# Masks of a block-sparse attention made later, new step tables for the attention and the first expert, and two pieces of weight work moved: fp32 attention and two MoE layers in one launch

## The chip, the cores and the metric

One NeuronCore of one Trainium2 chip runs the whole program. The metric is the device time of one execution in microseconds (us). Engines: PE multiplies matrices, DVE (VectorE), ACT (ScalarE) and POOL (GpSimd) work on vectors, SP issues the DMAs.

## The reference, cut to what matters

```
# attention: B=2, H=8, S=768, D=64; block 32, window 16
k_sum = max over each block of 32 keys;  v_sum = mean over each block of 32 values
scores_l = q @ k.T / 8, kept where |i-j| < 16
scores_s = q @ k_sum.T / 8 + log(32)
a = softmax([scores_l, scores_s]);  x = a @ [v, v_sum]         # 1536 rows of 512
h = x @ w_in (512x2048);  g = h - tanh(h);  x2 = g @ w_out (2048x512)
out = ((x2 @ w1) * (x2 @ w2)) @ w3 @ w_out2                    # 1024 wide, then 512
```

All is float32, and the weights arrive as 64-bit numbers.

## The kernel before, in words

**Products.** A float32 product is made as three reduced-precision ones (`split_mm`, L237 to L240): high x high, high x low, low x high. So every operand has a high part (a cast, `wh`, by ACT L193 or POOL L191) and a low part (a subtraction on POOL, `wl`, L200). A weight first comes in by DMA as `raw` (L126), and ACT (L145, sometimes also L149, the units listed in `PLAN["SIGN"]`) and DVE (L152 to L162) turn its 64-bit numbers into `dec`.

**Attention, 0 to about 118 us.** 24 groups g of 4 query tiles are in flight at once, as a pipeline of steps: S scores on PE (L428), M0 to M3 row maxima with a mask added (DVE, L438), E0 to E3 exponentials (ACT, L443), R one over the row sum (DVE, L450 and L451), PP the scaling of the probabilities `pr` (POOL, L455), T four transposes (PE, L462), PB their copy `pt` (ACT, L467), V the values `av` (PE, L477), XH and XL the two parts of the result (ACT, DVE). Every third group brings new keys (`key_blocks`, K0 to K2, block maxima on DVE L370 to L377, copied into the keys on POOL, L379), new values (`value_blocks`, on PE, from the rows of `mean`), their rows `vr` (ACT, L399) and their DMA into `vg` (BR, L404). Between these, PE makes the 32 parts of w3 @ w_out2 ahead of time: W0 and W1, `w34a`, each part two halves of three matmuls of 512 columns; the numbers of parts per step are in `PLAN["N34"]`. The tokens H, L, D, U and ST are pieces of the weights' decoding (cast, low part, one DVE operation, a whole unit, start of a unit).

No scheduler orders any of this. Each engine runs its instructions in the order in which the program writes them, and one that waits holds up all behind it. For the attention that order is written in `PLAN["L"]`, three lists of (token, lag), one for the first two steps, one until step 17, one after; a step g runs each token for group g minus its lag. Ahead of the steps the program calls `key_blocks(0, .)` and `scores(0)`; ahead of those again POOL makes the `mean` rows (L267 to L281) and three masks (L282 to L292) out of `band` (L258 to L265).

**First MoE, about 118 to 375 us.** `hidden` (ph), tanh, and the way back (x), 48 times; `PLAN["MIDDLE"]` sets the order inside a step, and its last row holds for all later ones.

**Second MoE.** For the first of three token blocks a loop over m = 0 to 7 makes a = x2 @ w1 (`product_a`), b and c = a*b (`product_b`), the high and low part of w3 @ w_out2 (`w34_split(m)`: cast `w34h` on ACT, `w34l` on POOL) and then adds the output product of the m before (`final`). The other two token blocks are made together, in seven products of halves instead of eight, for pairs of m (`group`, called for w1 and then for w2). A group runs products 1, 6, 5, then, at each `next(g)`, the output product that is pending (`between`) and 7, then 2, 4 and 3. After each DVE adds the bank `p_w` into a11, a12, a21, a22 (L900). `w_sums` makes the sums of weights that the next group multiplies with: up to its first `yield` `t_w` (two additions on DVE), up to its second `s_w` (four half-size ones on DVE, two casts on ACT L937, two low parts on POOL L243).

Of the kernel before, what the change touches and what calls it, by code (L numbers as in the profile page):

```python
# [21 lines left out]
P = 128  # L22
# [4 lines left out]
QT = 64  # L27
# [22 lines left out]
ALL = 4  # L50
FLUSH = 4

PLAN = {"cuts": [2, 17], "N34": [0, 0, 0, 0, 0, 2, 0, 2, 2, 0, 2, 1, 2, 1, 2, 0, 1, 2, 3, 1, 2, 1, 1, 3, 1, 2, 3],
        "MORE": (15, 18, 22), "MOREU": (20, 24, 32),
        "SIGN": (1, 3, 5, 7, 9, 11, 13, 14, 15, 17, 19, 20, 21, 22, 23, 24, 26, 27, 28, 29, 32, 35, 39, 41, 43, 45, 47, 49, 51, 53, 55, 57, 59, 61, 63, 65, 67, 69, 71, 73, 75, 77, 79), "ACT": (0, 4, 7, 8, 16, 19, 22, 25, 27, 28, 29, 31, 33, 35)}
PLAN["L"] = [
# [14 lines left out]
]  # L71
PLAN["MIDDLE"] = [
# [9 lines left out]
]  # L82
NEG = -8.0 * 1000000000.0
# [6 lines left out]
def fused_kernel(tc, qT, kT, vW, w_in, w_out, w1, w2, w3, wo2, out):  # L90
# [156 lines left out]
    with tc.tile_pool(name="base", bufs=1) as base, \  # L247
# [12 lines left out]
        for hf in range(2):  # L260
# [2 lines left out]
                                    fill=NEG, base=-1, channel_multiplier=-1)  # L263
            nc.gpsimd.affine_select(out=part, in_=part, pattern=[[-1, WK]], compare_op=ALU.is_ge,
                                    fill=NEG, base=2 * WIN - 1, channel_multiplier=1)  # L265

        mean = base.tile([P, 6 + BLK], F32, name="mean")  # L267
        nc.gpsimd.memset(mean, 0.0)

        def rows(col, a, b):  # L270

            nc.gpsimd.memset(col, 1.0 / BLK)
            for base_, step in ((-a, 1), (b - 1, -1)):
                nc.gpsimd.affine_select(out=col, in_=col, pattern=[[0, 1]], compare_op=ALU.is_ge, fill=0.0,
                                        base=base_, channel_multiplier=step)

        rest = base.tile([P, 1], F32, name="mean_rest")
        rows(mean[:, 6:7], WIN, WIN + BLK)
        rows(mean[:, 7:8], WIN + BLK, QT)
        rows(rest, CW, CW + WIN)  # L280
        nc.gpsimd.tensor_tensor(out=mean[:, 7:8], in0=mean[:, 7:8], in1=rest, op=ALU.add)  # L281
        masks = []  # L282
        for z in range(3):
            mk = base.tile([P, NC], F32, name=f"mask{z}")
            nc.gpsimd.memset(mk[:, BC], LOG_BLK)
            nc.gpsimd.tensor_copy(out=mk[:, :QT], in_=band[:, :QT])
            nc.gpsimd.tensor_copy(out=mk[:, CW:], in_=band[:, QT:])
            if z == 0:
                nc.gpsimd.memset(mk[:, :WIN], NEG)
            if z == 2:  # L290
                nc.gpsimd.memset(mk[:, NC - WIN:], NEG)
            masks.append(mk)  # L292

        w34 = [base.tile([P, DM], F32, tag=f"w34_{i}", name=f"w34_{i}") for i in range(NM)]
        xh = [base.tile([P, KC, TB], F32R, name=f"xh_{k}") for k in range(NTB)]
# [43 lines left out]
        with tc.tile_pool(name="p1", bufs=1) as p1, \  # L339
# [74 lines left out]
            def scores(g):  # L414

                nonlocal n_s
                n, u = divmod(g, NU)
                st[g] = []
                for _ in range(1 + (g >= ALL)):
                    tag = "extra" if g >= ALL and n_s % 3 == 2 else "s"  # L420
                    n_s += g >= ALL
                    st[g].append(ps1.tile([P, TU, NC], F32, tag=tag, bufs=2 if tag == "s" else 1, name=f"s_{g}_{n_s}"))
                wt.one = g >= ALL
                for i in range(TU):
                    t = u * TU + i
                    for hf in range(2):
                        r = slice(hf * QT, (hf + 1) * QT)
                        mm(out=st[g][i % len(st[g])][half_of(g, i, hf), i, :], lhsT=qt[n][r, t * QT:(t + 1) * QT],  # L428
                           rhs=kt[n][r, t * CW:t * CW + NC], start=True, stop=True)
# [78 lines left out]
            for i in range(3):  # L508
                key_blocks(0, i)
            scores(0)  # L510
            n34 = 0
            NN = B * NP
            done = set()
# [264 lines left out]
        def product_a(m, k):  # L778
            ph = half("w1", m, k)
            a = tmp("u", f"a_{m}_{k}")  # L780
            nc.scalar.copy(out=a, in_=ph)
            return a
# [193 lines left out]
        for m in range(1, NM):  # L976
            wt.high()
            wt.low()
            wt.start(min(2, len(wt.free) - (1 if m > 5 else (6 - m) // 2)))
            if m == NM - 1:  # L980
                assert len(wt.t) == len(wt.units)
                wt.free += [(rawp, "raw", "raw", NRAW)] * NRAW
                _, lhs = w_sums("w1", 0)
            a = product_a(m, 0)
            wt.unit(1)
            pb = half("w2", m, 0)
            c = product_b(m, 0, a, pb)
            wt.unit(1)
            if m == 1:
                resplit(4)  # L990
                resplit(4)
            if m == 4:
                for i in range(H):
                    x_sums(i)
            if m == 5:
                for i in (5, 6):
                    x_split(i, 0, nc.vector)
                    x_split(i, 1, nc.vector)
                wt.free += [(px, f"x{k}{c}", f"x{k}{c + 1}", 1) for k, c in ((1, 0), (2, H))]
            if m > 2:  # L1000
                wt.high()
                wt.low()
            w34_split(m)
            final(*prev)
            prev = m, 0, c
        todo, last = [(*prev, range(TB // P))], []
# [18 lines left out]
        for m in range(0, NM, 2):  # L1025
            pl_a, a12, a21 = wt.take(f"a_{m}", F32)
            pl_b, a22, b22 = wt.take(f"ab_{m}", F32)
            g = group("w1", m, lhs, a11, a12, a21, a22)
            next(g)
            sums = w_sums("w2", m)  # L1030
            next(sums)
            next(g)
            lhs = next(sums)
            for _ in range(3):
                next(g, None)
            pl_c, b12, b21 = wt.take(f"b_{m}", F32)
            b11 = tmp("u", f"b11_{m}")
            g = group("w2", m, lhs, b11, b12, b21, b22)
            next(g)
            more = m + 2 < NM  # L1040
            if more:
                sums = w_sums("w1", m + 2)
                next(sums)
            for a, b in ((a22, b22), (a11, b11), (a21, b21)):
                next(g)
                if more and a is a22:
                    lhs = next(sums)
                tt(a, a, ALU.mult, b)
            next(g, None)
            tt(a12, a12, ALU.mult, b12)  # L1050
            todo += [split_c(a11, m, 1), split_c(a21, m + 1, 1)]
            last += [split_c(a12, m, 2), split_c(a22, m + 1, 2)]
            wt.free += [pl_a, pl_b, pl_c]
# [56 lines left out]
```

## Time and profile before

| | |
|---|---|
| three runs, us | 574.33, 574.31, 571.29; median 574.31 |
| the profiled execution, us | 572.8, of it 571.1 the span of the engines' work |
| busy, us of the span | PE 556.0 (97%), DVE 456.1 (80%), ACT 335.1 (59%), POOL 292.0 (51%) |
| the chain that ended last | PE 81%, DVE 9%, issue 3%, ACT 3%, DMA 2% |
| granted PE clock, mean | 0.997 of full speed |

All times below are from the one profiled execution, in us from the start of the span. The page's 40 slices show PE at 6 tenths in the first two slices (14.3 us each), at 9 or more in every other one but the last, which holds the last copies and the DMAs of the output. The granted clock is at 8 tenths in the second slice and at 9 or more in all others.

### The profile page before, as it was taken

The page shows a single profiled execution, that of the slowest core. Times are in us where ns is not written, and L with a number is a line of the kernel's source. Part 1 is how long each engine was busy: PE and PEld are TensorE (multiplying, and loading weights), DVE is VectorE, ACT ScalarE, POOL GpSimd, SP SyncE. Part 2 cuts the span into 40 slices and gives each one's busy share as a digit, 9 for nine tenths or more (in the row PEclk, how much of TensorE's full clock was granted, in tenths as well). Part 3 has the DMA queues.
Part 4 walks back from the last instruction along what each step waited for, and adds up shares of the span by engine and source line. Part 5 has one row for each costly group of instructions (what it writes and reads, how often), then busy time and mean ns, then how long its engine had stood idle before and what let it go on. Part 6 is the DMA issues. An engine that isn't in the chain of part 4 may idle for free.

```text
span 571.1 us, 9225 instructions
## 1 busy us (share of the span) xinstructions
PE 556.0 (97%) x3224; PEld 450.0 (79%) x3224; DVE 456.1 (80%) x880; ACT 335.1 (59%) x739; POOL 292.0 (51%) x257
## 2 busy tenths in 40 slices
PE   6699999999999999999999999999999999999997
PEld 5477777778888888888888888888788877888885
DVE  4878899998899999889999769999378677868510
ACT  4799888876978876577766667845233321213110
POOL 4766775834464655535645315466536653617220
PEclk9899999999999999999999999999999999999999
DMA  8998777441232332122223003222000100000021
GB/s 329 352 312 287 279 242 231 143 146 38 74 111 76 110 100 84 37 84 87 88 82 102 1 2 110 75 73 75 0 1 1 74 1 1 1 0 1 1 92 55
DMA packets 18526, 56.56 MB, mean 99 GB/s; under 512 B 1968, under 2 KB 4656, under 8 KB 18480
## 3 DMA queue, kind: packets, MB, share of 16 engines
q1 hardware_dynamic: 18336, 55.84, 29.6%
q8 instruction: 25, 0.41, 0.3%
q14 instruction: 21, 0.17, 0.1%
q10 hardware_dynamic: 144, 0.13, 0.1%
HBM read 51.64 MB, written 3.15 MB: 96 GB/s over the span
## 4 chain that ended last, share of the span: by engine, by line
PE 81%; DVE 9%; issue 3%; ACT 3%; DMA 2%; SPq 1%; POOL 0%; DVEq 0%; ACTq 0%
PE ph L238 7%; PE ph L239 7%; PE ph L240 7%; PE x L238 7%; PE x L239 7%; PE x L240 7%; PE p_w L238 5%; PE p_w L240 5%; PE p_w L239 4%; PE o L240 4%; PE o L239 4%; PE o L238 4%; PE w34a L238 2%; DMA raw<-wo 2%; PE w34a L239 2%
## 5 line engine op out<-in xcount | busy, mean ns | idle before, releaser
L243 POOL TENSOR_TENSOR gl<-g,gh 128x512 fp32r<-128x512 f32 x48 | 65.0, 1354 | 127.1 <-ACT gh L729 69.4
L200 POOL TENSOR_TENSOR wl<-dec,wh 128x512 fp32r<-128x512 f32 x72 | 111.7, 1553 | 18.1 <-ACT wh L193 14.5
L238 PE MATMUL x<-gh,wh 128*128 128x512 f32 x192 | 74.9, 390 | 0.0
L238 PE MATMUL ph<-xh,wh 128*128 128x512 f32 x192 | 74.8, 390 | 0.0
L239 PE MATMUL x<-gl,wh 128*128 128x512 f32 x192 | 74.7, 389 | 0.0
L240 PE MATMUL ph<-xh,wl 128*128 128x512 f32 x192 | 74.7, 389 | 0.0
L239 PE MATMUL ph<-xl,wh 128*128 128x512 f32 x192 | 74.7, 389 | 0.0
L240 PE MATMUL x<-gh,wl 128*128 128x512 f32 x192 | 74.7, 389 | 0.0
L707 ACT ACTIVATE u<-ph 128x512 f32<-128x512 f32 x48 | 28.8, 600 | 52.0 <-PE ph L240 52.0
L162 DVE SCALAR_TENSOR_TENSOR dec<-raw,dec 128x512 uint32<-128x512 uint32 x48 | 48.6, 1013 | 1.5
L718 DVE TENSOR_TENSOR g<-ph,u 128x512 f32<-128x512 f32 x48 | 33.0, 687 | 17.6 <-ACT th L708 16.1
L720 DVE SCALAR_TENSOR_TENSOR g<-sq,g 128x512 f32<-128x512 f32 x48 | 45.3, 943 | 0.6 <-ACT sq L713 0.5
L243 POOL TENSOR_TENSOR s_w<-s_w,s_w 128x512 fp32r<-128x512 f32 x16 | 23.1, 1460 | 42.9 <-ACT s_w L937 23.2
L193 ACT CAST wh<-dec 128x512 fp32r<-128x512 f32 x54 | 33.7, 624 | 15.9 <-DVE dec L162 15.7
L238 PEld LDWEIGHTS x<-gh,wh 128*128 128x128 f32 x192 | 36.1, 188 | 7.9 <-DVE x2a L755 0.4
L443 ACT ACTIVATE pr<-pr,nm 128x120 f32<-128x120 f32 x96 | 37.9, 401 | 7.2 <-DVE nm L438 7.2
L240 PEld LDWEIGHTS x<-gh,wl 128*128 128x128 f32 x192 | 36.0, 188 | 7.5
L238 PEld LDWEIGHTS ph<-xh,wh 128*128 128x128 f32 x192 | 36.0, 188 | 7.5
L239 PEld LDWEIGHTS ph<-xl,wh 128*128 128x128 f32 x192 | 36.1, 188 | 7.4
L240 PEld LDWEIGHTS ph<-xh,wl 128*128 128x128 f32 x192 | 36.0, 188 | 7.5
L239 PEld LDWEIGHTS x<-gl,wh 128*128 128x128 f32 x192 | 36.0, 188 | 7.5 <-POOL gl L243 0.2
L724 DVE COPY_PREDICATED g<-mk,ph 128x512 f32<-128x512 uint32 x48 | 36.0, 749 | 3.9
(164 smaller groups left out, 1426.8 us busy)
## 6 DMA issues: line engine op xcount, KB each, us to landing
raw<-w SPq DMA_DIRECT2D x32, 512.0 KB
raw<-w_in SPq DMA_DIRECT2D x16, 512.0 KB
raw<-w_out SPq DMA_DIRECT2D x16, 512.0 KB
vg<-vW SPq DMA_DIRECT2D x8, 768.0 KB
raw<-wo SPq DMA_DIRECT2D x8, 512.0 KB
kt<-kT SPq DMA_DIRECT2D x7, 544.0 KB
qt<-qT SPq DMA_DIRECT2D x7, 384.0 KB
out<-u_out SPq DMA_DIRECT2D x6, 256.0 KB
```

The lines of the kernel that those rows point to most:

```text
L162: lambda tu=tu, su=su, lo=lo: stt(out=tu, in0=lo, scalar=29, in1=su, op0=ALU.logical_shift_right, op1=ALU.bitwise_or)])
L193: nc.scalar.copy(out=h, in_=self.t[n])
L200: nc.gpsimd.tensor_tensor(out=l, in0=self.t[self.n_low], in1=h[:, :].bitcast(F32), op=ALU.subtract)
L238: mm(out=acc, lhsT=lh, rhs=rh, start=start, stop=False)
L239: mm(out=acc, lhsT=lh, rhs=rl, start=False, stop=False)
L240: mm(out=acc, lhsT=ll, rhs=rh, start=False, stop=stop)
L243: eng.tensor_tensor(out=out, in0=x, in1=high.bitcast(F32), op=ALU.subtract)
L443: nc.scalar.activation(out=pr[g][:, i, :], in_=pr[g][:, i, :], func=AF.Exp, scale=-1.0, bias=nm[g][:, i:i + 1], accum_out=z[g][:, i, :1])
L707: nc.scalar.activation(out=u, in_=ph, func=AF.Square)
L718: nc.vector.tensor_tensor(out=gn, in0=ph, in1=u, op=ALU.mult)
L720: nc.vector.scalar_tensor_tensor(out=gn, in0=sq, scalar=GAM, in1=gn, op0=ALU.add, op1=ALU.mult)
L724: nc.vector.copy_predicated(out=gn, mask=mask[:, :].bitcast(U32), data=ph)
```

## The change

Four things. The masks and the rows of `mean` are made by the same POOL instructions, behind `key_blocks(0, .)` and `scores(0)` instead of ahead of them. The tables of `PLAN` are new: all three lists of `L`, the second cut (18 instead of 17), `N34`, `SIGN`, `ACT`, `MORE`, `MOREU` and the first eight rows of `MIDDLE`. `w34_split(m)` runs right behind `product_a` in the m loop, and the two calls ahead of its old place are gone. And in a group for w1, the sums for w2 begin behind the second `next(g)` instead of the first. The number of instructions of each kind stays, but for one more unit that is listed in `SIGN` (one ACT operation more, one DVE operation fewer).

```diff
-PLAN = {"cuts": [2, 17], "N34": [0, 0, 0, 0, 0, 2, 0, 2, 2, 0, 2, 1, 2, 1, 2, 0, 1, 2, 3, 1, 2, 1, 1, 3, 1, 2, 3],
+PLAN = {"cuts": [2, 18], "N34": [0, 0, 0, 0, 0, 1, 1, 2, 2, 0, 2, 1, 1, 1, 3, 0, 2, 1, 3, 0, 3, 1, 1, 3, 1, 2, 3],
...
@@ -264,33 +265,6 @@
             nc.gpsimd.affine_select(out=part, in_=part, pattern=[[-1, WK]], compare_op=ALU.is_ge,
                                     fill=NEG, base=2 * WIN - 1, channel_multiplier=1)
 
-        mean = base.tile([P, 6 + BLK], F32, name="mean")
-        nc.gpsimd.memset(mean, 0.0)
-
-        def rows(col, a, b):
-
-            nc.gpsimd.memset(col, 1.0 / BLK)
-            for base_, step in ((-a, 1), (b - 1, -1)):
-                nc.gpsimd.affine_select(out=col, in_=col, pattern=[[0, 1]], compare_op=ALU.is_ge, fill=0.0,
-                                        base=base_, channel_multiplier=step)
-
-        rest = base.tile([P, 1], F32, name="mean_rest")
-        rows(mean[:, 6:7], WIN, WIN + BLK)
-        rows(mean[:, 7:8], WIN + BLK, QT)
-        rows(rest, CW, CW + WIN)
-        nc.gpsimd.tensor_tensor(out=mean[:, 7:8], in0=mean[:, 7:8], in1=rest, op=ALU.add)
-        masks = []
-        for z in range(3):
-            mk = base.tile([P, NC], F32, name=f"mask{z}")
-            nc.gpsimd.memset(mk[:, BC], LOG_BLK)
-            nc.gpsimd.tensor_copy(out=mk[:, :QT], in_=band[:, :QT])
-            nc.gpsimd.tensor_copy(out=mk[:, CW:], in_=band[:, QT:])
-            if z == 0:
-                nc.gpsimd.memset(mk[:, :WIN], NEG)
-            if z == 2:
-                nc.gpsimd.memset(mk[:, NC - WIN:], NEG)
-            masks.append(mk)
-
         w34 = [base.tile([P, DM], F32, tag=f"w34_{i}", name=f"w34_{i}") for i in range(NM)]
         xh = [base.tile([P, KC, TB], F32R, name=f"xh_{k}") for k in range(NTB)]
         xl = [base.tile([P, KC, TB], F32R, name=f"xl_{k}") for k in range(NTB)]
@@ -508,6 +482,32 @@
             for i in range(3):
                 key_blocks(0, i)
             scores(0)
+            masks = []
+            for i in range(3):
+                mk = base.tile([P, NC], F32, name=f"mask{i}")
+                nc.gpsimd.memset(mk[:, BC], LOG_BLK)
+                nc.gpsimd.tensor_copy(out=mk[:, :QT], in_=band[:, :QT])
+                nc.gpsimd.tensor_copy(out=mk[:, CW:], in_=band[:, QT:])
+                if i == 0:
+                    nc.gpsimd.memset(mk[:, :WIN], NEG)
+                if i == 2:
+                    nc.gpsimd.memset(mk[:, NC - WIN:], NEG)
+                masks.append(mk)
+            mean = base.tile([P, 6 + BLK], F32, name="mean")
+            nc.gpsimd.memset(mean, 0.0)
+
+            def rows(col, a, b):
+
+                nc.gpsimd.memset(col, 1.0 / BLK)
+                for base_, step in ((-a, 1), (b - 1, -1)):
+                    nc.gpsimd.affine_select(out=col, in_=col, pattern=[[0, 1]], compare_op=ALU.is_ge, fill=0.0,
+                                            base=base_, channel_multiplier=step)
+
+            rest = base.tile([P, 1], F32, name="mean_rest")
+            rows(mean[:, 6:7], WIN, WIN + BLK)
+            rows(mean[:, 7:8], WIN + BLK, QT)
+            rows(rest, CW, CW + WIN)
+            nc.gpsimd.tensor_tensor(out=mean[:, 7:8], in0=mean[:, 7:8], in1=rest, op=ALU.add)
             n34 = 0
             NN = B * NP
             done = set()
@@ -982,6 +982,7 @@
                 wt.free += [(rawp, "raw", "raw", NRAW)] * NRAW
                 _, lhs = w_sums("w1", 0)
             a = product_a(m, 0)
+            w34_split(m)
             wt.unit(1)
             pb = half("w2", m, 0)
             c = product_b(m, 0, a, pb)
@@ -997,10 +998,6 @@
                     x_split(i, 0, nc.vector)
                     x_split(i, 1, nc.vector)
                 wt.free += [(px, f"x{k}{c}", f"x{k}{c + 1}", 1) for k, c in ((1, 0), (2, H))]
-            if m > 2:
-                wt.high()
-                wt.low()
-            w34_split(m)
             final(*prev)
             prev = m, 0, c
         todo, last = [(*prev, range(TB // P))], []
@@ -1027,9 +1024,9 @@
             pl_b, a22, b22 = wt.take(f"ab_{m}", F32)
             g = group("w1", m, lhs, a11, a12, a21, a22)
             next(g)
+            next(g)
             sums = w_sums("w2", m)
             next(sums)
-            next(g)
             lhs = next(sums)
             for _ in range(3):
                 next(g, None)
```

The new tables move instructions at these places. POOL at the start; `kt` is the keys with their block maxima, which the first scores read, `band` is what the masks are cut from, `pr` the probabilities. Before:

```order
L285 MEMSET mask_111 128x24
L286 COPY mask_111<-band 128x64
L287 COPY mask_111<-band 128x32
L291 MEMSET mask_111 128x16
L379 COPY kt_156<-kb_176 128x12x24
L455 TENSOR_TENSOR pr_189<-pr_189,r_248 128x480
```

Of the change:

```order
L265 AFFINE_SELECT band<-band 64x96
L263 AFFINE_SELECT band<-band 64x96
L265 AFFINE_SELECT band<-band 64x96
L353 COPY kt_129<-kb_149 128x12x24
L488 MEMSET mask_161 128x24
L489 COPY mask_161<-band 128x64
L490 COPY mask_161<-band 128x32
```

The copy of the first block maxima, which stood behind the last mask, now stands ahead of the first.

PE around the transposes T(3), with `w34a_0` and `w34a_1` the two halves of the first part of w3 @ w_out2, which come behind the second values V(1). Before:

```order
L477 MATMUL av_445<-pt_344,vg_164 64x64 x8
L238 MATMUL w34a_0_460<-wh_294,wh_321 128x512
L239 MATMUL w34a_0_460<-wl_295,wh_321 128x512
L240 MATMUL w34a_0_460<-wh_294,wl_322 128x512
L238 MATMUL w34a_1_464<-wh_294,wh_321 128x512
L239 MATMUL w34a_1_464<-wl_295,wh_321 128x512
L240 MATMUL w34a_1_464<-wh_294,wl_322 128x512
L462 MATMUL t_476<-ident,pr_311 120x128 x4
L428 MATMUL s_5_492<-kt_211,qt_274 64x120 x2
```

Of the change:

```order
L451 MATMUL av_440<-pt_343,vg_137 64x64 x8
L436 MATMUL t_455<-ident,pr_314 120x128 x4
L239 MATMUL w34a_0_461<-wh_284,wh_323 128x512
L240 MATMUL w34a_0_461<-wl_285,wh_323 128x512
L241 MATMUL w34a_0_461<-wh_284,wl_324 128x512
L239 MATMUL w34a_1_465<-wh_284,wh_323 128x512
L240 MATMUL w34a_1_465<-wl_285,wh_323 128x512
L241 MATMUL w34a_1_465<-wh_284,wl_324 128x512
L402 MATMUL s_5_485<-kt_209,qt_307 64x120 x2
```

T(3) moves from behind the part to ahead of it.

POOL between PP(1) (`pr_207`, after: `pr_204`) and PP(3) (`pr_311`, after: `pr_314`), with the casts and low parts of the first four decoded weights. Before:

```order
L455 TENSOR_TENSOR pr_207<-pr_207,r_291 128x480
L200 TENSOR_TENSOR wl_295<-dec_214,wh_294 128x512
L191 CAST wh_321<-dec_266 128x512
L200 TENSOR_TENSOR wl_322<-dec_266,wh_321 128x512
L455 TENSOR_TENSOR pr_245<-pr_245,r_337 128x480
L191 CAST wh_392<-dec_316 128x512
L200 TENSOR_TENSOR wl_393<-dec_316,wh_392 128x512
L191 CAST wh_414<-dec_362 128x512
L455 TENSOR_TENSOR pr_311<-pr_311,r_411 128x480
```

Of the change:

```order
L429 TENSOR_TENSOR pr_204<-pr_204,r_291 128x480
L201 TENSOR_TENSOR wl_285<-dec_214,wh_284 128x512
L192 CAST wh_323<-dec_260 128x512
L192 CAST wh_340<-dec_319 128x512
L429 TENSOR_TENSOR pr_244<-pr_244,r_345 128x480
L201 TENSOR_TENSOR wl_324<-dec_260,wh_323 128x512
L201 TENSOR_TENSOR wl_341<-dec_319,wh_340 128x512
L192 CAST wh_413<-dec_389 128x512
L429 TENSOR_TENSOR pr_314<-pr_314,r_418 128x480
```

Of the same work, two low parts instead of one now stand between PP(2) and PP(3).

## Rows read from the trace of the kernel before

**Rows 1.** Busy time by stage, all engines: PE, PEld, DVE, ACT, POOL, clock, DMA
```profile
20.00:30.00 10.00, 7.08 (x87) 5.38 (x88) 8.78 (x36) 8.08 (x32) 7.71 (x9) 0.83 1.02 339
60.00:80.00 20.00, 19.23 (x246) 14.47 (x246) 17.29 (x69) 18.65 (x64) 13.63 (x16) 1.00 0.77 264
200.00:300.00 100.00, 100.00 (x442) 82.51 (x441) 93.44 (x131) 69.69 (x123) 51.38 (x34) 1.00 0.27 81
```

**Rows 2.** Timeline of the first 12 us: start, length, engine, what, [idle before]
```profile
5.12 0.20 DVE L377 TENSOR_REDUCE kb<-hb 128x24 f32<-128x48 f32 x1
6.40 0.42 POOL L379 COPY kt<-kb 128x288 f32<-128x288 f32 x1
6.88 4.89 PE L428 MATMUL s<-kt,qt 64*64 64x120 f32 x48 [2.10 <-POOL kt L379]
```

**Rows 3.** The chain that ended last, then the timeline: what the first values wait for
```profile
6.80 12.26 DMA raw<-wo
...
19.31 0.69 PE L477 MATMUL av<-pt,vg 120*64 120x64 f32 x16 [0.64 <-DMA vg<-vr]
```

**Rows 4.** Timeline 21 to 30 us, POOL, then PE, around T(3)
```profile
21.61 0.99 POOL L455 TENSOR_TENSOR pr<-pr,r 128x480 f32<-128x480 f32 x1 [1.07 <-DVE r L451]
24.72 0.61 POOL L191 CAST wh<-dec 128x512 fp32r<-128x512 f32 x1
26.23 1.27 POOL L200 TENSOR_TENSOR wl<-dec,wh 128x512 fp32r<-128x512 f32 x1
...
26.20 0.80 PE L238 MATMUL w34a<-wh,wh 128*128 128x512 f32 x1
28.76 0.60 PE L462 MATMUL t<-ident,pr 128*120 128x128 f32 x4
```

**Rows 5.** PE and its granted clock, microsecond by microsecond
```profile
25.00:26.00 1.00, 0.86 (x16) 0.56 1.03 391
...
28.00:29.00 1.00, 1.00 (x6) 0.73 1.21 178
```

**Rows 6.** Timeline of PE: W then T then S; T then W then S
```profile
47.41 0.50 PE L238 MATMUL w34a<-wh,wh 128*128 128x512 f32 x1
...
48.92 0.60 PE L462 MATMUL t<-ident,pr 128*120 128x128 f32 x4
49.45 0.64 PE L428 MATMUL s<-kt,qt 64*64 64x120 f32 x16
...
95.79 0.65 PE L462 MATMUL t<-ident,pr 128*120 128x128 f32 x4
96.20 0.48 PE L238 MATMUL w34a<-wh,wh 128*128 128x512 f32 x1
...
97.77 0.64 PE L428 MATMUL s<-kt,qt 64*64 64x120 f32 x16
```

**Rows 7.** Timeline of PE at one output product that waits for w34l
```profile
406.65 0.39 PE L238 MATMUL o<-w34h,gh_c 128*128 128x512 f32 x1
407.22 0.50 PE L239 MATMUL o<-w34l,gh_c 128*128 128x512 f32 x1 [0.18 <-POOL w34l L243]
```

**Rows 8.** Timeline of PE, DVE, PE and POOL in the second pair's group for w1
```profile
472.98 0.39 PE L240 MATMUL p_w<-xh,s_w 128*128 128x512 f32 x1
...
472.98 1.75 DVE L900 TENSOR_TENSOR t_w<-wh,wl 128x512 f32<-128x512 f32 x2
...
474.65 0.68 DVE L900 TENSOR_TENSOR a<-a,p_w 128x512 f32<-128x512 f32 x1
...
475.70 0.39 PE L240 MATMUL p_w<-xh,wl 128*128 128x512 f32 x1
...
476.10 0.50 PE L238 MATMUL p_w<-xh,s_w 128*128 128x512 f32 x1
...
477.57 2.55 POOL L243 TENSOR_TENSOR s_w<-s_w,s_w 128x512 fp32r<-128x512 f32 x2 [4.00 <-ACT s_w L937]
...
478.96 0.40 PE L238 MATMUL p_w<-t,s_w 128*128 128x512 f32 x1
```

More of the change, by code (lines that the diff above doesn't have):

```diff
@@ L51 @@
 FLUSH = 4
-PLAN = {"cuts": [2, 17], "N34": [0, 0, 0, 0, 0, 2, 0, 2, 2, 0, 2, 1, 2, 1, 2, 0, 1, 2, 3, 1, 2, 1, 1, 3, 1, 2, 3],
-        "MORE": (15, 18, 22), "MOREU": (20, 24, 32),
-        "SIGN": (1, 3, 5, 7, 9, 11, 13, 14, 15, 17, 19, 20, 21, 22, 23, 24, 26, 27, 28, 29, 32, 35, 39, 41, 43, 45, 47, 49, 51, 53, 55, 57, 59, 61, 63, 65, 67, 69, 71, 73, 75, 77, 79), "ACT": (0, 4, 7, 8, 16, 19, 22, 25, 27, 28, 29, 31, 33, 35)}
+PLAN = {"cuts": [2, 18], "N34": [0, 0, 0, 0, 0, 1, 1, 2, 2, 0, 2, 1, 1, 1, 3, 0, 2, 1, 3, 0, 3, 1, 1, 3, 1, 2, 3],
+        "MORE": (15, 18, 22, 23, 24), "MOREU": (5, 13, 15, 20, 22, 25, 26),
+        "SIGN": (1, 2, 3, 5, 6, 7, 9, 11, 13, 15, 17, 18, 19, 20, 21, 22, 23, 24, 25, 27, 28, 29, 30, 31, 33, 34, 35, 37, 38, 39, 41, 43, 45, 47, 49, 51, 53, 55, 57, 59, 61, 63, 65, 67, 69, 71, 73, 75, 77, 79), "ACT": (0, 4, 8, 9, 16, 20, 22, 25, 26, 27, 29, 30, 31, 33)}
 PLAN["L"] = [
[14 rows of a table removed]
[15 rows of a table added]
 ]
 PLAN["MIDDLE"] = [
[8 rows of a table removed]
[8 rows of a table added]
     ["HID", "ST", "H", "EV", "C", "U", "UT", "G", "SM", "MM", "L", "RS", "BK"],
```

45 rows, old and new, of the table PLAN are left out of this document.

## Prediction

> **What bounds the kernel now.** First the page's table by engine and its 40 slices: PE is busy 97% of the span of 571.1 us, and all slices but the first two and the last stand at 9 tenths or more. So there is little to win, and the question is where PE still stands still, or does the same work in more time. Next the busy time by stage [rows 1]. The long middle gives the yardstick: between 200 and 300 us PE has 442 matmuls in 100 us, 0.226 us for one of 512 columns, with no idle time. From 20 to 30 us PE is idle 2.92 us, at a mean granted clock of 0.83; from 60 to 80 us it is idle 0.77, and there ACT is busy 18.65 of 20, so ACT is nearly a second bound. Then the timeline of the first 12 us [rows 2], the chain of waits and what the first values wait for [rows 3], the timeline around T(3) [rows 4], and the clock microsecond by microsecond [rows 5]. Last the timeline of PE at a few switches between kinds of work [rows 6], at one output product [rows 7] and in a group of seven products [rows 8].
>
> The sum is made against the profiled execution, 572.8, which lies 1.5 below the median of 574.31 and 1.5 above the lowest run, 571.29. Its mean with the three runs is 573.2, and that is what I carry the sum over to.
>
> **Masks and rows of means behind the block maxima.** The last block maximum is ready at 5.12 + 0.20 = 5.32 us, POOL copies it into the keys only at 6.40, and S(0) starts at 6.88, after a wait for that copy [rows 2]. All of 6.40 - 5.32 = 1.08 us is masks and mean rows, which go behind it. So S(0) comes up to 1.08 earlier. What takes it back: the third raw block is issued at 6.80 and lands 12.26 later, at 19.06, and the first values, behind it in the order of ACT and of the DMAs, start at 19.31 after a wait for their rows [rows 3]. In the new order of SP the same bytes are asked for in nearly the same order (one keys' and one values' transfer change places), and ACT still decodes that block ahead of the exponentials of groups 2 and 3. I therefore count **0** for the head start itself, with ends of 0 and -1.08. If that cover (the block's arrival) were gone, the whole 1.08 would show.
>
> **T(3) ahead of the first part of w34.** PE leaves V(1) at about 26.20 and goes into that part at once; T(3) runs at 28.76 [rows 4]. With the change T(3) comes first and waits for PP(3). POOL's PP(2) ends at 21.61 + 0.99 = 22.60. Behind it, up to PP(3), stood a cast, a low part and a cast; now two low parts and a cast: 22.6 + 2 x 1.27 + 0.61 + 0.99 = 26.7, and 0.2 for what PP(2) itself may start later, 26.9 for the end of PP(3) [rows 4]. So PE stands still from 26.20 to about 26.9, 0.7 us, and works without a gap from there. What it loses was cheap time: the clock was granted at 0.56 between 25 and 26 and at 0.73 between 28 and 29 [rows 5], so at or near its lower level, 1.2 GHz, in between, and the six matmuls of the part took 28.76 - 26.20 = 2.56 instead of 6 x 0.226 = 1.36 [rows 1, 4]. At half the rate 0.7 us is 0.35 us of full work if the clock rises when it did. I take **+0.4**, between 0 (PP(3) is there) and +2.1 (0.4, and a second low stretch that costs 1.7: half of the 3.4 us from about 25.1 to 28.5 which the rows show as low).
>
> The clock's row shows that it fell after PE had done little work since 21 us. The Trainium skill, *TensorE: Matmul & The Clock Gate*, section "HAM oscillation", says that a pause in TensorE's work lets the gate go back to half rate, so that the next burst starts cold; the trace agrees, with 0.56 in the microsecond when PE came back from waits. By that rule a longer pause ahead of T(3) is a case of its own, the first rival below.
>
> **Order inside the attention's steps.** V, W (a part), T, S becomes V, T, W, S. In the first form W takes 48.92 - 47.41 = 1.51 and T 49.45 - 48.92 = 0.53; in the second T takes 96.20 - 95.79 = 0.41 and W 97.77 - 96.20 = 1.57 [rows 6]: 2.04 against 1.98, 0.06 less. The new tables have T right ahead of W in 18 steps instead of 9: 9 x -0.06 = **-0.55**. W right behind another W costs 6 x 0.226 = 1.36 [rows 1] instead of some 1.5, in 4 steps instead of 2: 2 x -0.15 = **-0.3**. The ends of both together are 0 and -1.1. T now has one part of 1.5 us less ahead of it and asks for PP that much earlier; POOL's scaling took 0.99 [rows 4] and was done at least a microsecond before T in most steps, so what is late next is ACT's copy of T, on an engine that is 93% busy between 60 and 80 us.
>
> **Waits in that stretch.** There 0.77 us of PE is idle [rows 1]; with the tables' other order I take **-0.5**, between -0.95 (with the little of the stages beside it) and +1.0 (ACT, which gets one decoding operation more, becomes the bound: 0.05 of a 20 us stretch).
>
> **MIDDLE.** From 118 us to the second MoE PE stands still nowhere, and the eight new rows move ACT, DVE and POOL work under it: 0. The cover is the run of 0.226 us matmuls; were it gone in one step, a cast of 0.61 would show.
>
> **w34_split ahead of half w2.** In one output product the second matmul follows the first by 407.22 - 406.65 = 0.57 instead of 0.226, after a wait for `w34l` [rows 7]: 0.34. ACT's cast `w34h` stood behind that of c, which waits for DVE; now it is asked for ahead of it: **-0.35**. Ends 0 and -0.45. What is late next is the cast of c itself, which is needed only by the output product of the next m.
>
> **Sums of weights a step later.** In the group for w1, DVE makes `t_w` (1.75 from 472.98) ahead of the adds of product 7, whose last matmul starts at 472.98; those adds begin at 474.65, and PE, at product 3's place, waits for the second of them: 476.10 - 475.70 = 0.40 instead of 0.226 [rows 8]. With the adds first they run from about 473.45, so **-0.2** goes (ends 0 and -0.3). `t_w` then begins at 473.45 + 2 x 0.68 = 474.8 and ends after at most 1.75, between 476.1 and 476.55, where `s_w` began at about 476.0 before. POOL's first low part of `s_w` ends at 477.57 + 1.27 = 478.85; PE needs it for the third matmul of the next group's product, at 478.96 + 2 x 0.23 = 479.42 [rows 4, 8]. The slack is 0.57, and the delay is 0.1 to 0.55: it costs 0.
>
> **The sum:** 0 + 0.4 - 0.55 - 0.3 - 0.5 - 0.35 - 0.2 = -1.5, so 571.3 for the profiled execution and 573.2 - 1.5 = **571.7** as a median. About 0.5%, 2.9 us, is what a measurement of this kernel can tell from no change: faster is below 571.4, slower above 577.2.
>
> **Rivals.**
> - *A second low stretch of the clock* after the pause ahead of T(3). For it: the clock fell once already around 25 us, and the pause is 0.7 longer [rows 4, 5]. Against: T(3) and the part follow without a gap. The start then costs 2.1 instead of 0.4: 573.2 + 0.2 = 573.4. Chance 0.18.
> - *The sums of weights come late.* The slack of 0.57 decides: `t_w` begins 474.8 - 472.98 = 1.8 later, and if none of that is made up, PE waits 1.8 - 0.57 = 1.27 in each of four groups, 5.1 us, and the 0.2 isn't won: -1.3 + 5.1 = +3.8, so 577.0, slower than before. For it: DVE is one queue and `t_w` has 1.75 beside POOL's work; against: the adds that it lets pass would otherwise stand between `t_w` and `s_w`, so they are made up [rows 8]. Chance 0.08.
> - *The head start is real.* If the third raw block is decoded earlier or no longer ahead of what PE waits for [rows 3], the 1.08 shows, and T(3) finds PP(3) ready: -1.9 - 1.08 = -3.0, so 570.2. Chance 0.17.
> - *The tables do nothing.* If ACT, at 93%, is what paces 30 to 80 us [rows 1], the switches' 0.85 and the 0.5 come back as waits: -0.15, so 573.0. Chance 0.10.
>
> **How the numbers follow.** My forecast has 0.47. It is a sum of small terms with ends from -2.9 to +1, and the runs of before lie 3.0 us apart, so of its chance 0.24 falls below 571.4. With 0.15 of the head start that makes 0.39 for faster; slower is half of the late sums and a little of the clock, 0.06; the same has 0.55. The range goes from 569.2 (the head start and 1 us of the runs' spread) to 574.9 (the clock's case and 1.5 of the spread), which leaves out about 2 in 10.
>
> **What would show it.** S(0) would start near 5.8 and V(0) still near 19.3; POOL's PP(3) would end near 26.9 and T(3) start there, with PE gapless behind it and the clock low for no more than some 3 us. W would be 1.57 behind T and 1.36 behind W, and PE idle under 0.4 us from 60 to 80. The pitch at the output product and at product 3 would be 0.23. The prediction is wrong if V(0) moves ahead by a microsecond, if `p_w<-t,s_w` has waits on POOL, or if idle time of PE between 30 and 118 us is larger than before.

## The result and the profile after

| | before | after |
|---|---|---|
| six runs each, us | 571.29 to 574.33, median 573.38 | 579.78 to 582.13, median 580.64 |
| ratio of after to before | | 1.0144, 95% interval 1.0126 to 1.0162 |
| the profiled execution: span, us | 571.1 | 579.3 |
| PE busy, us of the span | 556.0 (97%) | 564.5 (97%) |

The change is slower: by 7.3 us, 1.3%, between the medians, by 1.4% as the ratio is taken, where I forecast 571.7 in a range up to 574.9. PE is as full as before: it has 8.5 us more of busy time for the same 3224 matmuls. The costliest groups on the page of after say where (line, engine, operation, out<-in, count, busy us, mean ns of one, idle before):

```profile
L239 PE MATMUL ph<-xh,wh 128*128 128x512 f32 x192 | 76.0, 396 | 0.5 <-DVE g L724 0.5
L241 PE MATMUL ph<-xh,wl 128*128 128x512 f32 x192 | 76.3, 397 | 0.0
...
L239 PE MATMUL x<-gh,wh 128*128 128x512 f32 x192 | 75.0, 390 | 0.0
```

The same three groups on the page of before:

```profile
L238 PE MATMUL ph<-xh,wh 128*128 128x512 f32 x192 | 74.8, 390 | 0.0
L240 PE MATMUL ph<-xh,wl 128*128 128x512 f32 x192 | 74.7, 389 | 0.0
...
L238 PE MATMUL x<-gh,wh 128*128 128x512 f32 x192 | 74.9, 390 | 0.0
```

A matmul of `ph` lasts 396 ns instead of 390, one of `x` 390 as before. By stage (the columns of [rows 1]), after:

```profile
20.00:30.00 10.00, 7.52 (x102) 5.74 (x106) 8.07 (x36) 9.88 (x35) 7.84 (x9) 0.80 0.83 286
...
60.00:80.00 20.00, 19.31 (x230) 14.23 (x228) 17.37 (x70) 18.22 (x61) 14.93 (x17) 1.00 0.82 270
...
100.00:120.00 20.00, 18.89 (x167) 14.34 (x165) 18.41 (x41) 14.04 (x39) 12.02 (x12) 1.00 0.45 140
120.00:140.00 20.00, 19.52 (x85) 15.51 (x84) 18.92 (x26) 13.81 (x26) 9.27 (x7) 1.00 0.30 90
...
200.00:300.00 100.00, 100.00 (x435) 81.21 (x434) 92.23 (x128) 67.15 (x120) 49.96 (x34) 1.00 0.26 83
```

and the two stages of before that stand in none of its rows ahead:

```profile
100.00:120.00 20.00, 19.81 (x173) 15.26 (x171) 18.91 (x46) 15.57 (x45) 15.46 (x14) 1.00 0.48 154
120.00:140.00 20.00, 20.00 (x89) 16.43 (x89) 16.90 (x27) 15.67 (x28) 9.17 (x7) 1.00 0.26 80
```

Between 200 and 300 us PE is gapless in both kernels, at a granted clock of 1.00 in both, and does 435 matmuls instead of 442 [rows 1]: 0.230 us for one instead of 0.226. That stretch is the one I had called "0". Ahead of it there are new gaps: PE is idle 1.11 and 0.48 us in 100 to 140, where before had 0.19 and none. Followed along the program, after is 0.2 us behind at T(7) (44.84 against 44.64) and 0.3 ahead at T(22) (108.24 against 108.58), with as many `w34a` matmuls done in both; it is 0.7 behind at the first `ph` and 1.7 behind ten microseconds later, and from there it loses steadily until it is 8.3 behind at the last product. The slower pitch is thus worth some 6.6 us, more than all the rest.

### The profile page after: what moved, and what is told of

It reads as the page before. It is cut to its first block, busy times and chain, and to the rows that moved or that the text cites. A ratio compares the mean times of both kernels' runs of the same rounds, so it can differ in the third digit from the quotient of the medians.

```text
span 579.3 us, 9222 instructions
## 1 busy us (share of the span) xinstructions
PE 564.5 (97%) x3224; PEld 451.0 (78%) x3224; DVE 456.0 (79%) x879; ACT 336.0 (58%) x740; POOL 291.1 (50%) x257
## 4 chain that ended last, share of the span: by engine, by line
PE 89%; DVE 4%; DMA 2%; issue 1%; SPq 1%; POOL 1%; ACT 1%; DVEq 0%
PE x L240 8%; PE x L239 8%; PE x L241 8%; PE ph L241 7%; PE ph L240 7%; PE ph L239 7%; PE p_w L239 5%; PE p_w L240 5%; PE p_w L241 5%; PE o L241 4%; PE o L240 4%; PE o L239 4%; PE w L239 3%; PE w L241 3%; PE w L240 3%; DMA raw<-wo 2%
## 5 line engine op out<-in xcount | busy, mean ns | idle before, releaser
L239 PE MATMUL ph<-xh,wh 128*128 128x512 f32 x192 | 76.0, 396 | 0.5 <-DVE g L724 0.5
L241 PE MATMUL ph<-xh,wl 128*128 128x512 f32 x192 | 76.3, 397 | 0.0
L240 PE MATMUL ph<-xl,wh 128*128 128x512 f32 x192 | 76.1, 396 | 0.0
L163 DVE SCALAR_TENSOR_TENSOR dec<-raw,dec 128x512 uint32<-128x512 uint32 x48 | 53.6, 1117 | 1.5
L720 DVE SCALAR_TENSOR_TENSOR g<-sq,g 128x512 f32<-128x512 f32 x48 | 47.5, 989 | 0.6 <-ACT sq L713 0.2
```

The lines of the kernel that those rows point to most:

```text
L163: lambda tu=tu, su=su, lo=lo: stt(out=tu, in0=lo, scalar=29, in1=su, op0=ALU.logical_shift_right, op1=ALU.bitwise_or)])
L239: mm(out=acc, lhsT=lh, rhs=rh, start=start, stop=False)
L240: mm(out=acc, lhsT=lh, rhs=rl, start=False, stop=False)
L241: mm(out=acc, lhsT=ll, rhs=rh, start=False, stop=stop)
L720: nc.vector.scalar_tensor_tensor(out=gn, in0=sq, scalar=GAM, in1=gn, op0=ALU.add, op1=ALU.mult)
```

## What the runs tell: the place of the tiles

The diff says nothing of it, but the change moves tiles. The masks and the mean rows were taken from `base` ahead of `w34`, `xh` and `xl`; now they are taken behind them. The built program's table of places (bytes in a partition) has:

```
                before   after
w34 (first)      19104   17472
xh_0             35488   33856
xl_2 (end)       84640   83008
raw (first)      84640   84640
wh_0            109216  109216
```

So `w34`, `xh` and `xl` lie 1632 bytes closer to the start, the masks and mean rows behind them, and all else where it was. Theory A: this costs the pitch. Rival B: the orders cost it. Four kernels, which differ from before or after in unused tiles alone:

```diff
 after_32:    after,  +base.tile([P, 8], F32) ahead of w34 and again behind xl
 before_0:    before, the same two
 before_all0: before, the one ahead of w34
 before_w0:   before, the one behind xl
```

**after_32.** 

> The changed kernel with two unused tiles of 32 bytes, ahead of the w34 tiles and behind xl, so that xh, xl and w34 start at 32 modulo 64 bytes again, as before; no instruction differs. Theory A (the change moved the masks' tiles behind xh and xl, and a product whose streamed operand starts at 0 modulo 64 takes 7 ns longer): the pitch of all products of the first MoE back at 0.227 us, 1140 x 0.007 = some 7.5 us gone, 572.5 to 574. Rival B (the new tables and orders cost the time, the place in memory nothing): 580.6 as the changed kernel, pitch of ph 0.234.

Measured 579.20, ratio 1.0109 (1.0092 to 1.0127): A in this form is wrong: the kernel is still 6.2 us slower than before (572.99 beside it).

**before_0.** 

> The kernel before with the same two unused tiles, which put xh, xl and w34 at 0 modulo 64 bytes; no instruction differs. A: 573.4 + 7.5 = 580 to 581, pitch of ph and w 0.234, of x 0.227. B: 573.4, pitch 0.227 everywhere.

Measured 580.76, ratio 1.0134 (1.0108 to 1.0160), without any instruction changed: the place in memory alone costs what the change lost. B falls as the whole cause.

**before_all0.** 

> The kernel before with one unused tile ahead of w34, which puts xh, xl and w34 and also the weights and most work tiles at 0 modulo 64. Theory A1 (a streamed operand at 0 is slow by itself): x is slow too, 2100 x 0.007 = +14, some 587. Theory A2 (it is slow only where the loaded weights stand at the other half of 64 bytes): pitch 0.227 everywhere, 573 to 574. B: 573.4.

Measured 572.83, ratio 0.9994 (0.9979 to 1.0010). With everything moved together by 32 bytes nothing is lost: here the place of a tile by itself doesn't matter.

**before_w0.** 

> The kernel before with one unused tile behind xl: xh and xl stay at 32, the weights' parts and most work tiles go to 0 modulo 64. A1: ph and w stay at 0.227, x (it streams weights, now at 0) goes to 0.234: 576 x 0.007 = +4, with some output products 577 to 579. A2: ph and w (streamed at 32, loaded at 0) at 0.234, x (both at 0) at 0.227: 573.4 + 6 = 579 to 580. B: 573.4.

Measured 579.59, ratio 1.0113 (1.0094 to 1.0132): A2, the relation between the streamed tile and the weights' tile, and not A1. What A2 had wrong was the 64 bytes, since after_32 has all its tiles at 32 modulo 64 and is slow. Its shift against the weights is 1632 + 32 = 1664 = 26 x 64, which is 128 modulo 256.

```profile
200.00:300.00 100.00, 100.00 (x434) 81.15 (x433) 92.17 (x129) 67.45 (x120) 49.32 (x34) 1.00 0.26 79
```

```profile
200.00:300.00 100.00, 100.00 (x442) 82.50 (x441) 93.55 (x130) 70.04 (x123) 51.41 (x34) 1.00 0.26 80
```

The first of these rows is before_w0's (434 matmuls), the second before_all0's (442).

The next three kernels put the change's tiles back and measure the modulus:

```diff
 after_place: after, mean, mean_rest and the masks taken ahead of w34 (filled where the change fills them)
 before_128:  before, +base.tile([P, 32], F32) behind xl
 before_256:  before, +base.tile([P, 64], F32) behind xl
```

**after_place.** 

> The changed kernel with the tiles of the masks and of the mean rows taken ahead of w34, xh and xl, as before, and filled where the change fills them; no instruction's order differs from the change. The runs so far: all tiles moved by 32 bytes together cost nothing (572.8), xh and xl moved by 32 against the weights cost 6.6 to 7.8, and a shift of 64 x 26 bytes (after_32) left 5.9 of the change's loss. Theory C (the streamed operand's start against the loaded weights' start counts, to more than 64 bytes): with the old distances the pitch of ph and w is 0.227 again and the whole loss of the first MoE goes; 571 to 574.5. Rival B (the order costs the 5.9 that after_32 left): 579 to 580.6.

Measured 573.64, ratio 1.0024 (1.0009 to 1.0040): the tiles' places are worth 6.5 to 7.0 of the 7.3 us (after less after_place, each against the runs of before beside it, or directly), and the rest of the change costs 0.2%.

**before_128.** 

> The kernel before with one unused tile of 128 bytes behind xl, so the weights' parts move by 128 bytes against xh and xl; no instruction differs. Theory C: slow as after_32, ph at 0.230 to 0.234, 577.5 to 580. Theory A2 (modulo 64 alone): 573 to 574. B: 573.4.

Measured 578.19, ratio 1.0093 (1.0072 to 1.0115): a distance of 128 bytes costs nearly as much as that of 224 in before_w0 (0.9% and 1.1%).

**before_256.** 

> The kernel before with one unused tile of 256 bytes behind xl. If the distance counts modulo 256: ph at 0.227, 573 to 574. If modulo 512 or more: ph at 0.230 to 0.234, 577.5 to 580. B: 573.4.

Measured 572.44, ratio 0.9990 (0.9974 to 1.0006). So it counts modulo 256. The stretch 200 to 300 us, of before_128 and then of before_256:

```profile
200.00:300.00 100.00, 100.00 (x436) 81.31 (x435) 92.44 (x129) 67.88 (x120) 49.70 (x35) 1.00 0.26 79
```

```profile
200.00:300.00 100.00, 100.00 (x442) 82.46 (x441) 93.49 (x131) 69.30 (x122) 51.43 (x34) 1.00 0.27 83
```

With the program's places and the trace's starts side by side, each of the 2160 products of 512 columns has a distance (start of the streamed operand minus start of the loaded weights, modulo 256) and a pitch (start of the next one minus its own, under 0.26 us, next one at the same distance, 130 to 560 us). Median over eleven kernels (these seven, before, after, before_px and best1):

```
distance mod 256      0    32    64    96   128   160   192   224
products          13598   101   200    42  1832   891   277  1874
median pitch, ns    227   234   231   232   232   234   233   234
```

In before 150 of the 2160 products are not at 0, in after 1238: 1088 more x 0.0064 (233.6 at the other distances in after less 227.2 at 0 in before, means) = 7.0 us. Why the distance counts, and whether it is the weights in use or those being loaded for the next product (the two lie on the same place modulo 256 in nearly all products), these runs don't tell.

**before_px** tests the rule forwards. The 150 products of before that are not at 0 all use a tile of `px`, and these lie 64 bytes off.

```diff
+        px.tile([P, 16], F32, tag="pad", name="pad")
```

> The kernel before with one unused tile of 64 bytes behind x2a, which puts the tiles of px, 64 bytes off the others modulo 256 before, to the same place modulo 256; no instruction differs. If the distance modulo 256 decides (theory C): the 150 products of the second MoE that have another distance fall from 0.234 to 0.227: 150 x 0.007 = -1.0, 571.9, and w and p_w at 0.227 from 437 us on. If not: 572.9.

Measured 571.35, ratio 0.9981 (0.9965 to 0.9997). In its trace product 1600 (counted from 0) and the last one start 127.9 us apart instead of 129.1.

## What the runs tell: the orders

**before_tables** is before with the new `PLAN` alone. 

> The kernel before with the new tables of PLAN alone; all tiles of base stay where they were. By the sum on record the tables give +0.4 at T(3), -0.85 by the order of T and W and -0.5 of waits: 572 to 573.5. From the trace of the change, whose first product of the first MoE starts 0.7 later although part 50 of w34 starts 1.3 earlier, and which loses another 1.2 up to 142 us: 574.5 to 575.5.

Measured 575.45, ratio 1.0043 (1.0024 to 1.0063): slower, where my sum had the tables at -0.95. Its PE rows with a wait on DVE in 116 to 130 us:

```profile
117.06 0.69 PE L478 MATMUL av<-pt,vg 120*64 120x64 f32 x16 [1.09 <-DVE xl L244]
...
126.83 0.50 PE L239 MATMUL ph<-xh,wh 128*128 128x512 f32 x1 [0.70 <-DVE g L725]
```

In before the first of them reads:

```profile
117.04 0.69 PE L477 MATMUL av<-pt,vg 120*64 120x64 f32 x16 [0.19 <-DVE xl L243]
```

The order did part of what I had worked out: with as many `w34a` matmuls done in both, before_tables is 0.4 ahead at T(7) (44.21 against 44.64) and 1.0 at T(22) (107.58 against 108.58). Then V(23) starts at 117.06, against 117.04. Both wait for the same thing, xl(22) on DVE, which ran from 116.59 in the one and 116.58 in the other: the lead became a wait. DVE shows why (start, length, what), in before:

```profile
116.58 0.41 DVE L243 TENSOR_TENSOR xl<-av,xh 128x256 fp32r<-128x256 f32 x1
116.91 1.43 DVE L160 SCALAR_TENSOR_TENSOR dec<-raw,dec 128x512 uint32<-128x512 uint32 x1
118.37 0.69 DVE L162 SCALAR_TENSOR_TENSOR dec<-raw,dec 128x512 uint32<-128x512 uint32 x1
...
122.74 0.68 DVE L718 TENSOR_TENSOR g<-ph,u 128x512 f32<-128x512 f32 x1
```

and in before_tables:

```profile
116.59 0.42 DVE L244 TENSOR_TENSOR xl<-av,xh 128x256 fp32r<-128x256 f32 x1
116.92 1.43 DVE L163 SCALAR_TENSOR_TENSOR dec<-raw,dec 128x512 uint32<-128x512 uint32 x1
118.27 0.41 DVE L159 TENSOR_SCALAR dec<-dec 128x512 uint32<-128x512 uint32 x1
118.72 0.69 DVE L161 SCALAR_TENSOR_TENSOR dec<-raw,dec 128x512 uint32<-128x512 uint32 x1
119.45 1.66 DVE L163 SCALAR_TENSOR_TENSOR dec<-raw,dec 128x512 uint32<-128x512 uint32 x1
...
124.07 0.68 DVE L719 TENSOR_TENSOR g<-ph,u 128x512 f32<-128x512 f32 x1
```

DVE has no gap in either stretch, and the new order has another 1.3 us of decoding ahead of the first `g` (124.07 instead of 122.74); the fourth hidden step needs its bank and waits 0.70.

**tables_nou**, `MOREU` cut to (5, 13, 15, 20). 

> The kernel before with the new tables, but MOREU cut to its first four steps, so that three whole units fewer are decoded by DVE in the last steps of the attention. In before_tables V(23) waits 1.09 us for xl and the fourth hidden step 0.70 for g, both on DVE. If those waits come from the units decoded early (theory G): they shrink under 0.3 each, 575.4 - 1.2 = 574.2 or better. If they come from the order of xl and g in the new rows themselves (rival H): they stay, 575.4; if the units then come late: over 576.

Measured 589.39, ratio 1.0292 (1.0274 to 1.0311). The waits of V(23) and `ph` go, but PE then waits 6.1 us at 135 for POOL's `wl` and again at 160 for ACT's `wh`, for weights that come late: these units can't be left for later.

**tables_u27**, `MOREU` with 27 for 25. 

> The kernel before with the new tables, but MOREU with 27 instead of 25, so that one whole unit is decoded behind the last xl but one instead of ahead of it. If DVE as a whole is the bound from 108 to 127 us (G2): V(23)'s wait of 1.1 goes and the fourth hidden step's wait grows by as much, 575.4. If the single xl is late because of its place (H): 575.4 - 1.1 = 574.3, and the second wait stays at 0.7.

Measured 574.41, ratio 1.0026 (1.0009 to 1.0044), not to be told from before_tables by time. In its trace V(23) waits no more, and the one wait left is

```profile
126.85 0.50 PE L239 MATMUL ph<-xh,wh 128*128 128x512 f32 x1 [1.92 <-DVE g L725]
```

1.92 instead of 1.09 + 0.70 = 1.79, and product 300 (counted from 0) starts at 143.35 instead of 143.31. The wait moved and the sum of both stayed, as G2 has it. But that DVE as a whole is the bound isn't shown, since DVE itself stands idle twice in this stretch:

```profile
115.31 0.43 DVE L244 TENSOR_TENSOR xl<-av,xh 128x256 fp32r<-128x256 f32 x1 [1.43 <-ACT xh L489]
...
124.08 0.69 DVE L719 TENSOR_TENSOR g<-ph,u 128x512 f32<-128x512 f32 x1 [0.61 <-ACT th L709]
```

The first `g` starts when it did in before_tables (124.07), now behind ACT's tanh, which came late behind a cast that had waited 2.42 us for DVE's decoding. What holds `g` is the order on DVE and ACT together.

**tables_oldmid**, the old `MIDDLE`. 

> The kernel before with the new tables for the attention, but the MIDDLE rows of before. If the 0.70 wait of the fourth hidden step comes from the new rows, which put DVE's work on one more unit ahead of the first g (theory G1): it goes, 575.4 - 0.7 = 574.7, and V(23) still waits 1.1 for xl. If DVE's backlog comes from the attention's lists (G2): the wait stays, 575.4.

Measured 575.05, ratio 1.0036 (1.0021 to 1.0051). G1 falls: with the old rows the second wait is larger, so here the new rows of `MIDDLE` help.

```profile
117.18 0.69 PE L478 MATMUL av<-pt,vg 120*64 120x64 f32 x16 [1.07 <-DVE xl L244]
...
127.88 0.50 PE L239 MATMUL ph<-xh,wh 128*128 128x512 f32 x1 [1.64 <-DVE g L725]
```

**before_masks** and **before_tail** are the other two parts alone, tiles in place. 

> The kernel before with the masks and mean rows filled behind the first block maxima, their tiles where they were. Theory D (the head start is taken back by the third raw block, as on record): 0, 572.9. Rival E (the head start of 1.08 shows): -1.1, 571.8. Rival F (PE starts earlier and then pauses longer, so that the clock is granted at its lower level for longer): +0.5 to +2, 573.4 to 575, with a granted clock under 0.8 somewhere between 10 and 40 us.

Measured 572.26, ratio 0.9998 (0.9985 to 1.0012): no difference in the time. In its one profile PP(0) starts at 11.75 instead of 12.76, so the head start is there; V(0) then waits 1.70 us for the DMA of its rows, where it waited 0.64 [rows 3], and starts no earlier (20.84, 19.31 before): there it is taken back, as forecast. The products from the first `ph` on come 0.5 earlier, less than executions with the same start differ by (see The clock below).

> The kernel before with w34_split behind product_a and the sums for w2 behind the second next, nothing else. By the sum on record -0.35 and -0.2, so 572.3, with no wait on POOL ahead of the output product and of product 3; by the rival on record (sums late) +5.1, 578.0.

Measured 572.60, ratio 0.9997 (0.9980 to 1.0014): no difference in the time; the trace shows a gain and a loss. The output product that waited for `w34l` [rows 7] runs at 0.23:

```profile
405.87 0.39 PE L238 MATMUL o<-w34h,gh_c 128*128 128x512 f32 x1
406.10 0.39 PE L239 MATMUL o<-w34l,gh_c 128*128 128x512 f32 x1
```

The sums that begin later win 0.23 at the product of [rows 8], but in the pair behind it they come late. The starts here are 0.30, 0.41 and 0.34 apart, where before has 0.23, and 0.5 us is lost; the weight loads there wait 0.4 for ACT's cast and 0.4 for POOL's low part of `s_w`, which they did nowhere in before:

```profile
502.46 0.47 PE L238 MATMUL p_w<-t,s_w 128*128 128x512 f32 x1
502.76 0.40 PE L239 MATMUL p_w<-t,s_w 128*128 128x512 f32 x1
503.17 0.50 PE L240 MATMUL p_w<-t,s_w 128*128 128x512 f32 x1
503.51 0.39 PE L238 MATMUL p_w<-t,s_w 128*128 128x512 f32 x1
```

**best1** joins the pad, which gained, and the two parts that cost nothing: before with masks late, w34_split and the sums moved, and the tile of `px`, without the tables. 

> The kernel before with the masks filled late (tiles in place), w34_split and the sums moved, and all large tiles at one place modulo 256, without the new tables. From single runs: -0.4 (masks), -0.4 in the trace (weight work), -1.1 (place): 572.6 - 1.9 = 570.7. If they do not add up: 571.3 to 572.6.

Measured 570.20, ratio 0.9957 (0.9937 to 0.9977), faster than both kernels. From 80 to 520 us its PE is idle 0.2 us in all. What it gains over the pad alone (0.9981) is not divided among its parts: masks and weight work alone came out at 0.9998 and 0.9997.

**best_place**, the changed kernel with its tiles in place and the tile of `px`. 

> The changed kernel with its tiles where they were before and the tiles of px at the same place modulo 256. Pitch 0.227 everywhere; after_place, 573.6, less the 1.1 of before_px: 572.5, about as the kernel before.

Measured 573.00, ratio 0.9991 (0.9972 to 1.0010).

## Why the prediction was wrong, point by point

- **"From 118 us to the second MoE PE stands still nowhere ...: 0".** This is the step that failed, and with it the first one, where the edit was no more than "masks and mean rows, which go behind" the copy of the block maxima. I priced instructions and waits. A pitch of 0.226 us was a yardstick to me and not a quantity that the change could move, and I did not ask where the tiles go when their creation moves. It cost some 7 of the 7.3 us: 1088 products at 0.2336 instead of 0.2272. No rival had it: they were about waits and the clock.
- **Order of T and W, -0.85, and waits, -0.5.** The order won some 0.55 from T(7) to T(22): before_tables goes from 0.43 to 1.00 ahead, after from 0.20 behind to 0.34 ahead. The waits did not go: from 60 to 80 us PE is idle 0.86 in before_tables and 0.69 in after, where it was 0.77 [rows 1]. And the lead did not last. I wrote that "what is late next is ACT's copy of T"; it was DVE's xl. The row was there: DVE was busy 18.91 of 20 us from 100 to 120 in before, and PE waited 0.19 for xl at its end. The tables came out at +2.6 instead of -0.95 in the medians; the traces show 1.0 of it (-1.0, then 1.0 and 1.0 given back in waits for DVE). The other 1.5 stays open: the profiled execution of before_tables is the fastest of its runs, and it is one of seven.
- **The start.** The block maxima are copied at 5.16 and S(0) starts at 5.96, as I said. V(0) was not earlier: it came at 21.79, and no longer behind its rows' DMA, but behind scores that waited 1.18 for DVE. PP(3) ended at 27.89, not 26.9, since PP(2) started at 22.73, 1.1 later than in before, where I had allowed 0.2; T(3) at 27.94 followed it at once, after a pause of 1.31 instead of 0.7. POOL, then PE, in after:

```profile
5.16 0.42 POOL L353 COPY kt<-kb 128x288 f32<-128x288 f32 x1 [2.29 <-DVE kb L351]
...
26.91 0.98 POOL L429 TENSOR_TENSOR pr<-pr,r 128x480 f32<-128x480 f32 x1
```

```profile
5.96 4.75 PE L402 MATMUL s<-kt,qt 64*64 64x120 f32 x48 [1.18 <-DMA qt<-qT]
...
14.94 1.11 PE L436 MATMUL t<-ident,pr 128*120 128x128 f32 x4 [2.76 <-POOL pr L429]
...
27.94 0.65 PE L436 MATMUL t<-ident,pr 128*120 128x128 f32 x4 [1.31 <-POOL pr L429]
28.35 0.47 PE L239 MATMUL w34a<-wh,wh 128*128 128x512 f32 x1
```

- **The clock.** My first rival had a pause ahead of T(3) bring the lower level again. In after it came earlier: PE had little to do from 12.2 to 14.94, since the new order puts PP(0) at 13.90 where it was at 12.76, and the clock was granted at 0.84, 0.50 and so on, at 1.2 GHz, from 13 to 24:

```profile
12.00:13.00 1.00, 0.18 (x6) 0.00 (x0) 0.68 (x2) 0.77 (x4) 0.00 (x0) 1.00 1.02 420
13.00:14.00 1.00, 0.00 (x0) 0.00 (x0) 0.97 (x4) 0.63 (x4) 0.10 (x1) 0.84 1.06 440
14.00:15.00 1.00, 0.06 (x1) 0.06 (x2) 1.00 (x5) 0.47 (x1) 0.88 (x1) 0.50 1.02 423
...
22.00:23.00 1.00, 1.00 (x19) 0.88 (x20) 0.62 (x6) 1.00 (x5) 0.84 (x2) 0.50 1.04 424
23.00:24.00 1.00, 1.00 (x18) 0.88 (x18) 1.00 (x7) 1.00 (x4) 1.00 (x2) 0.54 1.02 411
24.00:25.00 1.00, 1.00 (x20) 0.63 (x17) 0.62 (x4) 1.00 (x4) 1.00 (x1) 1.00 1.03 406
```

  The Trainium skill, *TensorE: Matmul & The Clock Gate*, section "HAM oscillation", says that what follows such a pause starts cold; the trace agrees, with 0.50 from 14 on. How much of this is the change's can't be told from one trace of each kernel. Eight kernels whose first 118 us have before's instructions in before's order (before, before_0, before_all0, before_w0, before_128, before_256, before_px, before_tail) show the lower level for 3.4 to 13.7 us in their one profile each, and their 25th `w34a` matmul starts anywhere from 39.08 to 41.25. After, with 10.2 us, has it at 40.49, inside that spread; after_place, where the lower level stood around T(3) (26.4 to 33.2), at 42.74, after_32 and best_place at 41.43 and 41.16. These four, with late masks and new tables together, average 1.5 later than the eight, which would cover the 0.2% that after_place left; that is argued, not shown.
- **w34_split, -0.35, and the sums, -0.2.** The first is right in the trace: between products 1400 and 1500 before_tail gains 0.45. The second is right at the product of [rows 8]: 0.23 between products 1700 and 1800, and in after product 3 of that group starts 0.23 after the matmul ahead of it instead of 0.40. But that isn't all: between 1800 and 1900 before_tail loses 0.5, the rival of late sums, in one pair and at a tenth of the price that I gave it. In after it did not come.

```profile
482.98 0.39 PE L241 MATMUL p_w<-xh,wl 128*128 128x512 f32 x1
483.21 0.40 PE L239 MATMUL p_w<-xh,s_w 128*128 128x512 f32 x1
```

- **The signs I had named.** Of those for being wrong, one came in after: PE is idle 1.97 us from 30 to 120, where before had 1.06. Another, waits on POOL at `p_w<-t,s_w`, came in before_tail and not in after. Of those for being right, two failed in after beside those of the start: PE idle 0.69 instead of under 0.4 from 60 to 80, and a low clock of 10.2 us instead of some 3. None of them points at the 7 us, which have no idle time in them.

## What to carry to other kernels

When a diff moves where tiles are allocated, compare their places in the built program before pricing instructions, and read the pitch of the main matmul (count in a gapless stretch) in both traces first: it is one number and stands for hundreds of microseconds. Keep all large operands of such products (512 columns of four bytes) at one place modulo 256 bytes; here a pad of 64 bytes won 0.2% by itself. A gain on the bound engine is kept only if what it waits for next comes earlier too: follow it to the first wait that ends at the same time in both traces.

## What the runs showed that I had not expected

A product of 512 columns of four bytes takes 227 ns when the streamed operand and the loaded weights start at the same place modulo 256 bytes, and 231 to 234 ns at each of the seven other distances in steps of 32 that occurred. Moving both together by 32 bytes changes nothing (572.83 against 572.99). And DVE's instructions of one line, L163, `dec<-raw,dec`, took 0.68 and 1.66 us within ten microseconds of before_tables (109.53 and 113.95). POOL's `wl` ran beside the three long ones (from 113.65, 116.34 and 119.08) and not beside that short one, but another short one of the same line, at 112.06, had a `wl` beside it (from 111.61); what makes the difference was not tried.
